# Denominators and three heads' numerators in one product, the general path off SyncE's queue, and the first loads in other halves

## The chip, the cores and the metric

The kernel runs on one core of one Trainium2 chip. The metric is the device time of one execution in microseconds; the kernel before has a median of 270.71 us over 3 runs (270.58 to 271.08). The engines are TensorE (PE in the profile; PEld is its weight load), VectorE (DVE), ScalarE (ACT), GpSimd (POOL) and SyncE (SP), which here only issues DMAs and waits.

## The reference

All arrays are bf16. The input x has 2048 rows of 512. Two branches are computed from it and mixed by a gate per row.

```python
x = A_x
g = _sigmoid((x * gate_w).sum(-1, keepdims=True))
a = _A_ref(x, A_wq, A_wk, A_wv, A_wo, A_beta)
b = _B_ref(x, B_w_gate, B_w_up, B_w_down)
return g * a + (1 - g) * b
```

Branch B is a gated feed-forward block: gelu(x w_gate) times (x w_up), 1792 wide, then w_down. Branch A is attention with a memory, 32 heads of 16 dimensions, over four segments of 512 rows:

```python
logits = jnp.einsum('bhqd,bhkd->bhqk', qs, ks) * scale + mask
p = _softmax(logits, axis=-1)
a_dot = jnp.einsum('bhqk,bhkd->bhqd', p, vs)
pq = phi(qs)
num = jnp.einsum('bhld,bhde->bhle', pq, M)
den = jnp.einsum('bhld,bhd->bhl', pq, z)[..., None] + 1e-06
a_mem = num / den
o = g * a_mem + (1.0 - g) * a_dot
...
pk = phi(ks)
M = M + jnp.einsum('bhld,bhle->bhde', pk, vs)
z = z + jnp.einsum('bhld->bhd', pk)
```

Here phi(t) is t + 1 for positive t and exp(t) otherwise, the mask is causal within the segment, and g is a sigmoid of one beta per head. The first segment has an empty memory.

## The kernel before, in words

The kernel keeps the transposed x of a segment (512 features over 128 partitions and four chunks `fc`, by 512 rows) and forms from it K, Q (transposed, eight heads in each of four groups `c`), V, the gate and the up branch. Every such product is one unit of TensorE work: four matmuls of 512 columns into one PSUM bank, followed by one read of the bank by VectorE or ScalarE. The pool `gen` has four such banks for all units; four more banks hold the logits. Attention runs in 72 visits: in each, `group_qk` (L612) forms 2048 columns of logits, ScalarE takes their exponential, GpSimd masks the diagonal blocks, and two visits after its last block a group's `pv` (L632) multiplies by V into a pair of banks, which VectorE transposes, normalises and turns back.

The order of all other work is made at build time by a planner. Streams of units (K, Q, V, gate, up, down, output, memory) carry a wanted visit, a condition, and a cost in TensorE and VectorE time; `fill_to` (L746) takes the unit with the smallest wanted visit, corrected by a modelled backlog of VectorE, until the next exponential is due. `later(n, f)` (L312) runs a step n visits on, and `passed(pe, dve)` (L692) books its modelled time. Each engine then executes its instructions in the order in which they were written down.

The memory: after a segment, `u_pk` (L386) transposes phi(K) by DMA, `u_M` (L523) adds phi(K)ᵀ[V 1] to the accumulator `Macc`, and `u_mask` (L542) writes the block-diagonal copies: `Mz` (8 columns per group, for the denominators) and, two and eight visits later, the halves of `Mn` (128 columns per group, eight heads of 16). `u_den` (L563) multiplies phi(Q) by `Mz` for two groups at a time, eight matmuls of 8 columns into one bank `zd`; VectorE adds 1e-6 out of the bank at once, and one visit later `f_inv` takes the reciprocal and multiplies by g. `mem_num` (L596) multiplies phi(Q) of one group by `Mn`, four matmuls of 128 columns into a bank `mn`; VectorE multiplies by the reciprocals into `tm`, and a DMA on SyncE's queue transposes it for `add_mem`. This is done for three segments and four groups.

The head: `load_inputs` (L134) issues on SyncE's queue x's first segment in two halves, wk in two halves of its columns, wq, the gate vector, wv and the gate weights. `transpose_x0` (L175) transposes x on TensorE; VectorE and ScalarE copy it out. Then, before the planner starts, three K units, four Q units, the gate vector's transpose, four V units and the gate units follow one another. Each of the first three K units is cast by VectorE, which also writes its two masked copies `KTm` (L378); VectorE casts Q and V too.

The end: the kernel has a general path (`general`, L1066) for inputs whose logits could overflow. A flag `safe` is computed from absolute maxima; its value is loaded into a register of every engine at L1129, and all engines branch at L1130. In this execution the general path is not taken. Its DMAs (x, transposes, V, output) are all on SyncE's queue.

```python
    ok = nc.values_load(safe[0:1, 0:1])
    with tc.If(ok == 0, preferred_fallthrough_block=True, label="safe"):
        general()
```

Of the kernel before, what the change touches and what calls it, by code (L numbers as in the profile page):

```python
# [11 lines left out]
ALU = mybir.AluOpType  # L12

P = 128
D = 512
# [15 lines left out]
DV = HV * DH  # L31
BF = dt.bfloat16
# [21 lines left out]
def kernel(  # L54
# [47 lines left out]
    Mn = [const([P, NC8, 128], BF, f"Mn{i}") for i in range(2)]  # L102
    Mz = [const([P, NC8, 8], BF, f"Mz{i}") for i in range(2)]
# [23 lines left out]

    def x_seg(s):
        nc.sync.dma_start_transpose(xS[s % NX][:, :, :], x2[s * L:(s + 1) * L, :])
# [45 lines left out]
    def transpose_x0():  # L175
        for half in range(2):
            for f0 in range(0, FC, 2):
                T = pgen.tile([P, 1024], BF, name="x0T", tag="gen")
                for i in range(4):
# [3 lines left out]
                dst = xS[0][:, f0:f0 + 2, half * 256:half * 256 + 256].rearrange(  # L183
                    "q f (p k) -> q f k p", k=2)
                src = T[:, 0:512].rearrange("q (f k p) -> q f k p", f=2, k=2)
# [177 lines left out]

    def u_k(s, c):
        def f():
            T = gen("kT")
            for fc in range(FC):
                nc.tensor.matmul(T[:, :], lhsT=wk[:, fc, c * P:(c + 1) * P],  # L368
                                 rhs=xS[s % NX][:, fc, :],
                                 start=(fc == 0), stop=(fc == FC - 1))  # L370
                if fc < FC - 1:
                    yield MM512
            cast(ktb[:, c, :], T[:, :])
            if general_now[0]:
                return MM512
            for p in range(2):
                eng = nc.vector if s == 0 and c < NK else nc.gpsimd
                eng.tensor_scalar(out=KTm[:, (NC8 * s + c) % NK, :, p, :],  # L378
                                  in0=ktb[:, c, :].rearrange("q (b k) -> q b k", b=NB),
                                  scalar1=eo[:, p:p + 1], scalar2=None, op0=ALU.mult)  # L380
            return MM512
        return 4 * MM512, EVAC, f

    pk_at = {}

    def u_pk(s, c):  # L386
        def f():
            assert ("k", s, c - c % 2) in ready
            nc.sync.dma_start_transpose(pk[:, :, c * P:(c + 1) * P], ktb[:, c, :])
# [55 lines left out]
    def u_vs(s):  # L445
        def f():
            v, w = V[s % 2], Vs[s % 2]
            nc.sync.dma_start(w[0:64, :, 0:VE], v[64:128, :, 0:VE])
            nc.sync.dma_start(w[64:128, :, 0:VE], v[0:64, :, VE:2 * VE])
# [55 lines left out]
    def u_out(s, qt):  # L505
        def f():
# [12 lines left out]
            nc.sync.dma_start(out2[q0:q0 + P, :], osb)  # L519
# [22 lines left out]
    def u_mask(s):  # L542
        def half(h0):
            nc.vector.tensor_tensor(
                out=Mn[s % 2][:, h0:h0 + 2, :].rearrange("p c (h e) -> p c h e", h=8),
# [5 lines left out]
        def f():  # L551
# [3 lines left out]
            nc.vector.tensor_tensor(out=Mz[s % 2][:, :, :], in0=Macc[:, :, :, 16],  # L555
# [6 lines left out]

    def u_den(s, pair):  # L563
        def f():
            assert general_now[0] or ("q", s, 2 * pair) in ready
            T = gen("zd")
            Tv = T[:, 0:KT * 16].rearrange("p (q h) -> p q h", q=KT)
            for cc in range(2):
                c = 2 * pair + cc
                for qq in range(KT):  # L570
                    nc.tensor.matmul(Tv[:, qq, 8 * cc:8 * cc + 8],
                                     lhsT=pq[:, c, qq * P:(qq + 1) * P],
                                     rhs=Mz[s % 2][:, c, :], start=True, stop=True)
# [4 lines left out]
            nc.vector.tensor_scalar_add(r, Tv, 1e-6)  # L578

            def f_inv():  # L580
# [4 lines left out]
                passed(0.0, 0.8)  # L585
# [7 lines left out]

    tms = {}

    def mem_num(s, c):  # L596
        assert general_now[0] or (count(("Mn", s)) > c // 2 and count(("inv", s)) > c // 2)
        T = gen("mn")
        for qq in range(KT):
            nc.tensor.matmul(T[:, qq * P:(qq + 1) * P],  # L600
                             lhsT=pq[:, c, qq * P:(qq + 1) * P], rhs=Mn[s % 2][:, c, :],
                             start=True, stop=True)
        tm = wk2.tile([P, KT, 8, DH], BF, name="tm", tag="tm")
# [556 lines left out]
```

## Time and profile before

| | |
|---|---|
| median of 3 runs | 270.71 us (270.58 to 271.08) |
| the profiled execution | 270.57 us, of which span 268.84 us |
| TensorE busy | 262.3 us (98%), granted clock 0.996 |
| VectorE, ScalarE, GpSimd busy | 203.7 (76%), 209.0 (78%), 156.8 us (58%) |
| first K product starts | 5.83 us, after a wait for wk |
| numerators L600 | 48 of 128 columns; multiply L604 12 times 686 ns |
| denominators L571 | 48 of 8 columns |
| last VectorE instruction of the output | ends 265.4 us |
| end of the span | 268.8 us |

Times are microseconds from the start of the span unless marked ns. In a timeline line the first number is the start and the second the time until the last instruction of the merged group ended, so a group of pipelined matmuls is longer than its starts are apart; the bracket gives the idle time before it and what ended that. In a view of one source line, the three numbers after the count are the shortest, median and longest duration in ns, followed by the first and last start. A q behind an engine's name marks its instruction queue: waits, branches and DMA issues.

### The profile page before, as it was taken

To read this page: it belongs to the slowest core of one execution; us is meant where nothing else is said; L and a number is where in the kernel's file an instruction comes from. 1 tells how busy PE (TensorE), PEld (TensorE's weight loads), DVE (VectorE), ACT (ScalarE), POOL (GpSimd) and SP (SyncE) were. 2 spreads that over 40 slices of the span, in tenths; PEclk is the share of its full clock that TensorE was granted. 3 is DMA by queue.
4 is the path that set the end of the run, shared out by engine and by line. 5 is a ranking of instruction groups with operands and counts; after the bars stand their busy time and mean duration, and the time that the engine had idled before them with its cause. 6 is when DMAs were issued, how large, how long until landed. Compare 5 with 4: busy or idle time off the path is not lost.

```text
span 268.8 us, 6576 instructions
## 1 busy us (share of the span) xinstructions
PE 262.3 (98%) x2713; PEld 117.5 (44%) x2713; DVE 203.7 (76%) x390; ACT 209.0 (78%) x163; POOL 156.8 (58%) x298
## 2 busy tenths in 40 slices
PE   7999999999999999999999999999999999999993
PEld 3454434344453444445444444444444544344441
DVE  2999575868777887697986979596898588697374
ACT  3237889999997998889999988889888987567420
POOL 4000168897905979987811998596875089654400
PEclk9999999999999999999999999999999999999998
DMA  6999901200160000301052002110000200001102
GB/s 205 334 211 321 331 18 35 41 4 0 29 136 2 0 22 22 78 4 41 0 68 56 2 21 50 33 34 8 20 24 21 66 2 20 19 3 41 39 22 85
DMA packets 30282, 16.60 MB, mean 62 GB/s; under 512 B 20008, under 2 KB 28968, under 8 KB 30248
## 3 DMA queue, kind: packets, MB, share of 16 engines
q1 hardware_dynamic: 30248, 16.14, 22.9%
q8 instruction: 22, 0.36, 0.6%
q14 instruction: 12, 0.10, 0.1%
HBM read 8.14 MB, written 2.10 MB: 38 GB/s over the span
## 4 chain that ended last, share of the span: by engine, by line
PE 86%; POOL 5%; issue 4%; DMA 2%; ACT 1%; SPq 0%; DVE 0%; ACTq 0%; DVEq 0%; POOLq 0%
PE gT L456 19%; PE uT L477 17%; PE dT L493 14%; PE lg L618 8%; PE od L643 6%; PE aT L510 5%; PE qT L282 5%; PE kT L368 5%; PE vT L397 4%; POOL pT L627 3%; POOL KTm L378 2%; DMA wk<-in_A_wk_dram 2%; PE MT L531 1%; PE mn L600 1%; ACT pT L623 1%
## 5 line engine op out<-in xcount | busy, mean ns | idle before, releaser
L627 POOL TENSOR_SCALAR_AFFINE_SELECT pT<-pT 64x256 bf16<-64x256 bf16 x256 | 113.8, 445 | 94.2 <-ACT pT L623 81.4
L623 ACT ACTIVATE pT<-lg 128x2048 bf16<-128x2048 f32 x72 | 135.1, 1876 | 24.9 <-PE lg L618 21.6
L477 PE MATMUL uT<-x,wup 128*128 128x512 bf16 x224 | 60.4, 380 | 0.0
L456 PE MATMUL gT<-x,wga 128*128 128x512 bf16 x224 | 57.0, 380 | 0.0
L493 PE MATMUL dT<-wdn,G 128*128 128x512 bf16 x224 | 52.9, 380 | 0.0
L483 DVE TENSOR_TENSOR G<-uT,G 128x512 bf16<-128x512 f32 x56 | 38.1, 684 | 6.4 <-PE uT L477 6.2
L378 POOL TENSOR_SCALAR KTm<-ktb,eo 128x512 bf16<-128x512 bf16 x26 | 40.6, 1572 | 1.3
L650 DVE STREAM_TRANSPOSE oq<-od 128x512 f32<-128x512 f32 x32 | 21.0, 695 | 19.5 <-PE od L643 19.5
L493 PEld LDWEIGHTS <-G 128*128 128x128 bf16 x224 | 20.8, 98 | 25.0 <-issue 2.1
L456 PEld LDWEIGHTS <-wga 128*128 128x128 bf16 x224 | 20.5, 98 | 23.9 <-issue 2.2
L477 PEld LDWEIGHTS <-wup 128*128 128x128 bf16 x224 | 19.8, 97 | 24.0 <-issue 5.4
L618 PE MATMUL lg<-QT,KTm 32*128 32x192 bf16 (+7 forms) x512 | 28.5, 287 | 0.0
L305 DVE CAST G<-gT 128x512 bf16<-128x512 f32 x24 | 16.5, 688 | 9.7 <-PE gT L456 9.5
L618 PEld LDWEIGHTS <-KTm 32*128 32x128 bf16 x512 | 8.3, 92 | 28.4 <-issue 28.1
L643 PE MATMUL od<-pT,V 64*32 64x128 bf16 (+7 forms) x512 | 19.4, 284 | 0.2 <-POOL pT L627 0.2
L643 PE MATMUL od<-pT,Vs 64*32 64x128 bf16 (+7 forms) x512 | 19.4, 284 | 0.0
L471 ACT ACTIVATE G<-G 128x3584 bf16<-128x3584 bf16 x6 | 18.8, 3182 | 0.0
L656 DVE SCALAR_TENSOR_TENSOR o<-oq,ogs,rden 128x256 bf16<-128x256 f32 x32 | 17.0, 532 | 1.1
L368 PE MATMUL kT<-x,wk 128*128 128x512 bf16 x64 | 16.8, 380 | 0.9 <-DMA wk<-in_A_wk_dram 0.9
L282 PE MATMUL qT<-x,wq 128*128 128x512 bf16 x64 | 16.6, 379 | 0.0
L515 DVE SCALAR_TENSOR_TENSOR tB<-aT,gct,tB 128x512 bf16<-128x512 f32 x16 | 11.9, 746 | 6.0 <-PE aT L510 5.7
L510 PE MATMUL aT<-wo,oT 128*128 128x512 bf16 x64 | 16.5, 380 | 0.0
(96 smaller groups left out, 274.8 us busy)
## 6 DMA issues: line engine op xcount, KB each, us to landing
out_dram<-tB SPq DMA_DIRECT2D x16, 128.0 KB, 1.7
wup<-in_B_w_up_dram SPq DMA_DIRECT2D x1, 1792.0 KB, 8.4
wdn<-in_B_w_down_dram SPq DMA_DIRECT2D x1, 1792.0 KB
wga<-in_B_w_gate_dram SPq DMA_DIRECT2D x1, 1280.0 KB, 10.2
Vs<-V SPq DMA_DIRECT2D x8, 144.0 KB, 2.6
G<-in_A_x_dram SPq DMA_DIRECT2D x2, 256.0 KB, 2.8
wk<-in_A_wk_dram SPq DMA_DIRECT2D x2, 256.0 KB, 4.2
wq<-in_A_wq_dram SPq DMA_DIRECT2D x1, 512.0 KB, 5.7
```

Of the source, the lines that this page charges most:

```text
L282: nc.tensor.matmul(T[:, :], lhsT=wq[:, fc, c * P:(c + 1) * P], rhs=xS[s % NX][:, fc, :], start=(fc == 0), stop=(fc == FC - 1))
L368: nc.tensor.matmul(T[:, :], lhsT=wk[:, fc, c * P:(c + 1) * P], rhs=xS[s % NX][:, fc, :], start=(fc == 0), stop=(fc == FC - 1))
L378: eng.tensor_scalar(out=KTm[:, (NC8 * s + c) % NK, :, p, :], in0=ktb[:, c, :].rearrange("q (b k) -> q b k", b=NB), scalar1=eo[:, p:p + 1], ...
L456: nc.tensor.matmul(T[:, :], lhsT=wga[:, fc, hs * P:(hs + 1) * P], rhs=xS[s % NX][:, fc, :], start=(fc == 0), stop=(fc == FC - 1))
L477: nc.tensor.matmul(T[:, :], lhsT=wup[:, fc, hs * P:(hs + 1) * P], rhs=xS[s % NX][:, fc, :], start=(fc == 0), stop=(fc == FC - 1))
L483: nc.vector.tensor_tensor(out=g, in0=T[:, :], in1=g, op=ALU.mult)
L493: nc.tensor.matmul(T[:, :], lhsT=G[s % NG][:, hs, qt * P:(qt + 1) * P], rhs=wdn[:, hs, :], start=(hs == 0), stop=(hs == HS - 1))
L510: nc.tensor.matmul(T[:, :], lhsT=oT[:, fc, qt * P:(qt + 1) * P], rhs=wo[:, fc, :], start=(fc == 0), stop=(fc == FC - 1))
L618: nc.tensor.matmul(lg[:, j, off:off + n], lhsT=KTm[rows, i % NK, b].rearrange("r p k -> r (p k)"), rhs=QT[rows, i % NC8, 64 * b:L], start= ...
L623: nc.scalar.activation(pT[:, :, :], lg[:, :, :], AF.Exp, scale=DH ** -0.5)
L627: nc.gpsimd.affine_select(out=v, in_=v, pattern=[[0, 4], [1, 64]], compare_op=ALU.is_ge, fill=0.0, base=0, channel_multiplier=-1)
L643: nc.tensor.matmul(od[p][32 * j:32 * j + 32, 64 * b:L], lhsT=w[:, 18 * h:18 * h + 32], rhs=t[rows, j, off:off + n], start=(b == 0), stop=( ...
```

## The change

- One tile `Mm` of 8 + 128 columns per group takes the place of `Mz` and `Mn`. `u_den` multiplies phi(Q) by the first 56 columns (`DN`: eight denominators and the numerators of `HD` = 3 heads) for two groups, eight matmuls of 56 columns in one bank; `mem_num` multiplies by the other 80 columns (five heads).
- `f_inv`, after the reciprocals, also multiplies the three heads' numerators of both groups out of the `zd` bank into two tiles `tm`; `mem_num` multiplies the other five heads into the same tile.
- The stream of denominators also waits until the mask's half is written and the numerators of the earlier pair are done.
- In the general path x, V and the output go through GpSimd's DMA queue, and TensorE transposes take the place of the transposing DMAs; SyncE issues nothing there, and the flag is loaded by the other four engines only.
- x's first segment is loaded with 128 consecutive rows over the partitions, two rows of 1 KB per partition and half instead of 2 KB in one piece; the copies after the transpose are contiguous. wk is loaded in two halves of its rows (1 KB pieces) instead of its columns (512 B pieces).
- `first_k` runs the first three K units together: first the products of chunks 0 and 1 for all three, then chunks 2 and 3, each followed by its casts.

```diff
+HD = 3
+DN = 8 + HD * DH
...
-    Mn = [const([P, NC8, 128], BF, f"Mn{i}") for i in range(2)]
-    Mz = [const([P, NC8, 8], BF, f"Mz{i}") for i in range(2)]
+    Mm = [const([P, NC8, 8 + 128], BF, f"Mm{i}") for i in range(2)]
...
             nc.sync.dma_start(x0[:, 2 * i:2 * i + 2, :],
-                              x2[half * i:half * (i + 1), :].rearrange("(p k) d -> p k d", p=P))
+                              x2[half * i:half * (i + 1), :].rearrange("(k p) d -> p k d", p=P))
         for i in range(2):
-            n = slice(D // 2 * i, D // 2 * (i + 1))
-            cols(wk[:, :, n], A_wk[:, n])
+            cols(wk[:, 2 * i:2 * i + 2, :], A_wk[D // 2 * i:D // 2 * (i + 1), :])
...
+    def first_k():
+        Ts = [gen("kT") for c in range(NK)]
+        for c in range(NK):
+            for _ in k_part(Ts[c], 0, c, range(0, FC // 2)):
+                pass
+        for c in range(NK):
+            for _ in k_part(Ts[c], 0, c, range(FC // 2, FC)):
+                pass
+            k_done(Ts[c], 0, c)
+
+    def turn(dst, src):
+        T = pgen.tile([P, 1024], BF, name="tT", tag="gen")
+        for i in range(KT):
+            nc.tensor.transpose(T[:, i * P:(i + 1) * P], src[:, i, :], ident[:, :])
+        nc.vector.tensor_copy(dst, T[:, 0:512].rearrange("p (i t) -> p i t", i=KT))
...
             T = gen("zd")
-            Tv = T[:, 0:KT * 16].rearrange("p (q h) -> p q h", q=KT)
+            Tv = T[:, 0:2 * KT * DN].rearrange("p (c q e) -> p c q e", c=2, q=KT)
             for cc in range(2):
                 c = 2 * pair + cc
                 for qq in range(KT):
-                    nc.tensor.matmul(Tv[:, qq, 8 * cc:8 * cc + 8],
+                    nc.tensor.matmul(Tv[:, cc, qq, :],
                                      lhsT=pq[:, c, qq * P:(qq + 1) * P],
-                                     rhs=Mz[s % 2][:, c, :], start=True, stop=True)
+                                     rhs=Mm[s % 2][:, c, 0:DN], start=True, stop=True)
...
-                passed(0.0, 0.8)
+                for cc in range(2):
+                    c = 2 * pair + cc
+                    t = wk2.tile([P, KT, 8, DH], BF, name="tm", tag="tm")
+                    tmp[(s, c)] = t
+                    scale(t, Tv[:, cc, :, 8:], s, c, 0, HD)
+                passed(0.0, 1.4)
...
+    def scale(t, src, s, c, h0, h1):
+        nc.vector.tensor_tensor(
+            out=t[:, :, h0:h1, :], in0=src.rearrange("p q (h d) -> p q h d", d=DH),
+            in1=rdm[s % 2][:, :, 8 * c + h0:8 * c + h1, None].to_broadcast((P, KT, h1 - h0, DH)),
+            op=ALU.mult)
...
-            nc.tensor.matmul(T[:, qq * P:(qq + 1) * P],
-                             lhsT=pq[:, c, qq * P:(qq + 1) * P], rhs=Mn[s % 2][:, c, :],
+            nc.tensor.matmul(Tv[:, qq, :],
+                             lhsT=pq[:, c, qq * P:(qq + 1) * P], rhs=Mm[s % 2][:, c, DN:],
                              start=True, stop=True)
...
+        tm = tmp.pop((s, c))
+        scale(tm, Tv, s, c, HD, 8)
...
-    for c in range(NK):
-        run(u_k(0, c))
+    first_k()
...
-                    lambda s=s, pair=pair: ("q", s + 1, 2 * pair) in ready)
+                    lambda s=s, pair=pair: ("q", s + 1, 2 * pair) in ready and
+                    count(("Mn", s + 1)) > pair and count(("num", s + 1)) == 2 * pair)
...
     def general():
         general_now[0] = True
+        queue[0] = nc.gpsimd
...
-    ok = nc.values_load(safe[0:1, 0:1])
+    ok = nc.values_load(safe[0:1, 0:1],
+                        engines=[mybir.EngineType.PE, mybir.EngineType.DVE,
+                                 mybir.EngineType.Activation, mybir.EngineType.Pool])
```

More of the change, by code (lines that the diff above doesn't have):

```diff
@@ L362, in u_phk, with k_part, k_done @@
         return 0.0, 0.0, f
+    def k_part(T, s, c, fcs):
+        for fc in fcs:
+            nc.tensor.matmul(T[:, :], lhsT=wk[:, fc, c * P:(c + 1) * P], rhs=xS[s % NX][:, fc, :],
+                             start=(fc == 0), stop=(fc == FC - 1))
+            if fc < FC - 1:
+                yield MM512
+    def k_done(T, s, c):
+        cast(ktb[:, c, :], T[:, :])
+        if general_now[0]:
+            return
+        for p in range(2):
+            eng = nc.vector if s == 0 and c < NK else nc.gpsimd
+            eng.tensor_scalar(out=KTm[:, (NC8 * s + c) % NK, :, p, :],
+                              in0=ktb[:, c, :].rearrange("q (b k) -> q b k", b=NB),
+                              scalar1=eo[:, p:p + 1], scalar2=None, op0=ALU.mult)
     def u_k(s, c):
@@ L366, in f @@
             T = gen("kT")
[L367 to L380, printed above, removed]
+            yield from k_part(T, s, c, range(FC))
+            k_done(T, s, c)
             return MM512
         return 4 * MM512, EVAC, f
+    def first_k():
[12 more added lines that the diff above has]
+        nc.vector.tensor_copy(dst, T[:, 0:512].rearrange("p (i t) -> p i t", i=KT))
     pk_at = {}
@@ L942, in can_num @@
     def can_num(s, c):
-        if count(("den", s)) <= c // 2 and ("q", s, c - c % 2) in ready:
+        if (count(("den", s)) <= c // 2 and ("q", s, c - c % 2) in ready and
+                count(("Mn", s)) > c // 2):
             need(("den", s), c // 2 + 1)
@@ L1073, in general @@
             if s % NX == 0:
-                x_seg(s)
+                rows = G[(s + 1) % NG][:, 0:KT, :]
+                nc.gpsimd.dma_start(rows, x2[s * L:(s + 1) * L, :]
+                                    .rearrange("(k p) d -> p k d", p=P))
+                for fc in range(FC):
+                    turn(xS[s % NX][:, fc, :].rearrange("p (k t) -> p k t", k=KT),
+                         rows[:, :, fc * P:(fc + 1) * P])
             for c in range(NC8):
```

44 lines of the change are left out of this document (25 added, 19 removed).

## The prediction

> **What bounds the kernel now.** I read the page first (busy shares, slices), then the chain that ended last, then the timeline of the three places that the change touches: the first 17 us, the memory products, the last 4 us.
>
> ```profile
> PE 262.3 (98%) x2713; PEld 117.5 (44%) x2713; DVE 203.7 (76%) x390; ACT 209.0 (78%) x163; POOL 156.8 (58%) x298
> PE   7999999999999999999999999999999999999993
> ```
>
> TensorE is busy 98% of the span; only its first slice and its last slice have holes. In the list of waits TensorE waits for another engine between 12 and 265 us never longer than 0.2 us at a time. So from about 12 us on, whatever delays TensorE or shortens its work moves the end one for one, until another engine becomes late.
>
> The head, from the timeline:
>
> ```profile
> 5.83 2.76 PE L368 MATMUL kT<-x,wk 128*128 128x512 bf16 x12 [0.91 <-DMA wk<-in_A_wk_dram]
> 6.90 0.69 DVE L305 CAST ktb<-kT 128x512 bf16<-128x512 f32 x1 [1.18 <-PE kT L368]
> 7.63 0.62 DVE L378 TENSOR_SCALAR KTm<-ktb,eo 128x512 bf16<-128x512 bf16 x2
> ...
> 8.50 3.63 PE L282 MATMUL qT<-x,wq 128*128 128x512 bf16 x16
> ...
> 10.66 2.48 DVE L305 CAST QT<-qT 128x512 bf16<-128x512 f32 x4
> ...
> 12.17 1.31 PE L397 MATMUL vT<-wv,x 128*128 128x448 bf16 x6
> ```
>
> TensorE starts K when wk lands, and from 6.90 us VectorE works without a pause (cast, two masked copies, three times over, then the Q casts). There are four PSUM banks for all of this; the ninth tile, the first vT, takes the bank of the second qT, whose cast ends at 10.66 + 0.60 + 0.68 = 11.95 us. vT starts at 12.17: VectorE is only 0.2 us ahead of TensorE here.
>
> The memory products, from the timeline:
>
> ```profile
> 74.96 0.65 PE L413 MATMUL zT<-wv,x 128*128 128x65 bf16 x16
> 75.45 0.34 PE L571 MATMUL zd<-Mz,pq 128*128 128x8 bf16 x8
> 75.65 1.24 PE L456 MATMUL gT<-x,wga 128*128 128x512 bf16 x5
> ...
> 97.28 0.39 PE L600 MATMUL mn<-Mn,pq 128*128 128x128 bf16 x4
> ...
> 97.50 0.38 PE L368 MATMUL kT<-x,wk 128*128 128x512 bf16 x1
> ```
>
> Starts tell the pace: 16 products of 65 columns in 0.49 us (30 ns each), 8 of 8 columns in 0.20 us (25 ns), 4 of 128 columns in 0.22 us (56 ns).
>
> The end, from the views of lines 1129, 1130 and 1155, and of SyncE's waits:
>
> ```profile
> L1129 SPq TENSOR_LOAD <-safe x1: 543/543/543, 265.8 to 265.8; - x1
> L1130 SPq COMPARE_BRANCH  x1: 58/58/58, 266.4 to 266.4; - x1
> L1130 SPq EVENT_SEMAPHORE  x8: 17/17/17, 266.9 to 267.5; - x8
> L1155 SPq EVENT_SEMAPHORE  x10: 17/28/28, 267.5 to 268.8; - x10
> SPq L1130 <- SPq L1130: 0.5, 1, 0.5
> ```
>
> After the last output DMA (issued at 265.41, 0.33 us long) SyncE alone is still walking: flag load, branch, 0.5 us of nothing, eight steps of DMA semaphores for the path not taken, then the closing waits. The other engines are through the branch by 266.7 us.
>
> **The change part by part.** The sum is made against the profiled execution: 270.57 us (span 268.84 and 1.73 around it), 0.14 below the median of the three runs (270.71).
>
> *56 and 80 columns.* 48 pairs (3 segments, 4 groups, 4 tiles of queries) of 25 + 56 = 81 ns become 56 + 80 columns. 56 lies between the rows of 8 and 65 columns (25 to 30 ns), I take 27; 80 lies between 65 and 128 (30 to 56), by a straight line 36. So 63 ns, and 48 x 18 = 0.86 us less on TensorE, which is the path. Bounds: 55 ns (-1.25 us) and 86 ns (+0.24).
>
> *More, smaller VectorE multiplies.* 12 products of 512 elements (0.686 us each) become 12 of 192 and 12 of 320. The casts out of PSUM took 0.28 us at 128 elements, 0.62 at 448 and 0.69 at 512, which gives 0.35 and 0.48: 0.15 us more each, 1.8 us in all. VectorE is idle 24% of the time, so I cost it at nothing; without that cover it is +1.8.
>
> *The held bank.* Before, the zd bank is free after the add (0.2 us). Now it holds three heads' numerators until the multiplies that follow the reciprocal, which is emitted one visit later: den and reciprocal stood 6.6, 6.2, 4.3, 2.6, 1.6 and 2.0 us apart (75.4 to 82.1, 108.9 to 115.1, 143.8 to 148.1, 173.4 to 175.9, 202.5 to 204.1, 237.7 to 239.7). For that time three banks are left. I laid TensorE's tiles against the ends of their reads. In five windows three banks hold all that is alive. In the second an od pair (PV at 112.1 us) takes two at once: the gT at 113.63 would wait for the first od transpose (114.08), 0.45 us, and the uT at 115.79 for the cast behind the reciprocal, about 0.4. That is 0.85 us for a window with a PV in it. The planner now books 1.4 instead of 0.8 for the reciprocal's step and may place units otherwise, so I take 0.5; bounds 0 and 2.6 (three windows). The den's new conditions (mask done, two numerators done) were met in all six places already, and the numerators' transposing DMAs had landed before the next multiplies; nothing there waits longer.
>
> *Loads.* x's first halves go from 2 KB to 1 KB packets, wk's halves from 512 B to 1 KB. The DMA view gave 367 GB/s in the stretch of x (2.4 to 3.4 us), 268 in that of wk (4 to 5) and 331 in that of wq (6.2 to 8.4, 1 KB). So x's 512 KB lands 0.15 us later, each wk half is 0.19 shorter: first half at 5.78 + 0.15 - 0.19 = 5.74, second about 6.33, wq about 8.24 instead of 8.46. The transposed copies are done at 5.62 and 5.82 and become contiguous, so they are no later. TensorE starts K about 0.05 us sooner (bounds: 0.3 sooner, 0.15 later).
>
> *K in halves of the contraction.* The 12 products (0.216 us apart) end at 8.37 instead of 8.43. But the first K tile is finished by the eighth product instead of the fourth: 4 x 0.216 = 0.86 us later. VectorE's unbroken row starts at 5.78 + 7 x 0.216 + 0.38 + 0.04 = 7.71 instead of 6.90 and reaches the end of the second Q cast 5.05 us later, at 12.76. vT then starts at about 12.78 instead of 12.17: +0.6 us, and behind it VectorE keeps ahead again (0.6 us per cast against 0.76 per vT). Bounds: +0.35 with wk early, +0.75 with x late, and -0.1 if the bank does not bind.
>
> *The end without SyncE.* The flag load (0.54), branch (0.06), gap (0.47) and eight steps (0.6) leave SyncE's queue; what then holds its closing waits is the last output's landing, 1.7 us after 265.41 = 267.1. POOL gets the steps of its own DMA queues (the output, Vs and x rows of the general path are now its): from 266.46, eight more of 0.07 to 0.09 us, so 267.1 too. SyncE gets some four more closing waits of 0.06. It reaches its first drain at about 267.5 instead of 268.03: -0.55 us. Bounds: -0.85 (all waits met by 267.1) and +0.3 (POOL's branch over a longer block takes TensorE's 0.39 us instead of 0.05). No transfer of this execution changes its queue.
>
> Sum: 270.57 - 0.86 + 0.5 + 0.6 - 0.55 = 270.26, say 270.3 us.
>
> **The rivals.**
> 1. *The head loses nothing.* If K starts 0.3 us sooner or the ninth tile finds another bank, the head gives about -0.1. For it: TensorE did wait 0.91 us for wk. Against it: the wait of vT on VectorE's count and only 0.2 us of room. With a held bank costing 0.2: 270.57 - 0.86 + 0.2 - 0.1 - 0.55 = 269.3.
> 2. *The held bank decides.* Place: a PV pair inside a window; price 0.85 us each. From 1.7 us on, two windows, the kernel is slower by over 0.2% (-0.86 + 0.6 - 0.55 + 1.7 = +0.9). With three: 270.57 - 0.81 + 2.55 = 272.3. For it: VectorE is already the late one in such stretches (a uT finished at 113.8 was read until 116.6), and its step grows by 0.7 us. Against it: only one of six windows had a PV inside.
> 3. *The columns' split gives nothing on TensorE*, because the spacing includes the load of new weights (98 ns each, in front of every product) and is a straight line in the columns; then 8 + 128 costs what 56 + 80 does, and the time is 270.26 + 0.86 = 271.1. The rows of 25, 30 and 56 ns speak against it: 8 columns and 65 differ by 5 ns only, 65 and 128 by 26. The Trainium skill, TensorE: Matmul & The Clock Gate, section Back-to-back issue gap, gives such a line for a stream of loads and products, 81 ns at 128 columns and 131 at 512; by it the estimate is 146 ns for either pair. The trace has 56 and 216 and does not agree.
>
> **How the numbers follow.** A measurement of this kernel can tell about 0.2%, 0.54 us, from no change. My forecast gets 0.42 (own range 269.6 to 271.0; faster 0.13, same 0.24, slower 0.05), rival 1 0.30 (all faster), rival 2 0.22 (all slower), rival 3 0.06 (same 0.04, slower 0.02). Together faster 0.43, same 0.28, slower 0.29. The range leaves out what of rival 1 adds the 55 ns pair and of rival 2 more than three windows, under 0.2 in all: 269.0 to 272.3.
>
> **What would show it.** Right: products of 56 and 80 columns at 27 and 36 ns; the first K cast near 7.7 us and vT near 12.8; SyncE without flag load and branch, its first drain near 267.5 less what the rest moved. Wrong: vT before 12.3 us (the head gains); holes in TensorE between den and the multiplies in more than one window; POOL's branch longer than 0.3 us; a different order of units between visits that makes VectorE late elsewhere.

## The result, and the profile after

The changed kernel takes 272.61 us (median of six runs, 272.15 to 272.79); the kernel before, run beside it, 271.02 us (270.58 to 271.15). The ratio is 1.0055, with a 95% interval of 1.004 to 1.007: 1.6 us slower. The profiled execution of the changed kernel took 272.53 us with a span of 270.70, against 270.57 and 268.84.

The page of the changed kernel, busy shares and TensorE's slices:

```profile
PE 258.4 (95%) x2674; PEld 117.6 (43%) x2713; DVE 204.7 (76%) x404; ACT 207.7 (77%) x161; POOL 157.0 (58%) x298
PE   7899999999999999999999999999999999999993
```

The page hardly tells that anything happened. (TensorE's busy sum is no measure here: 39 product records are missing from this trace, as the two counts show.) VectorE's share is still 76%, though its 203.7 us became 204.7 and its instructions 390 became 404. So the places have to be looked at one by one, those of the prediction first.

The first 14 us, from the timeline of the changed kernel:

```profile
6.04 2.76 PE L367 MATMUL kT<-x,wk 128*128 128x512 bf16 x12 [0.63 <-DMA wk<-in_A_wk_dram]
7.97 0.69 DVE L306 CAST ktb<-kT 128x512 bf16<-128x512 f32 x1 [2.20 <-PE kT L367]
8.64 3.63 PE L283 MATMUL qT<-x,wq 128*128 128x512 bf16 x15
11.73 2.48 DVE L306 CAST QT<-qT 128x512 bf16<-128x512 f32 x4
12.47 0.16 PE L194 MATMUL gwT<-ident,G 4*128 4x4 bf16 x1 [0.20 <-DVE QT L306]
13.07 3.19 PE L422 MATMUL vT<-wv,x 128*128 128x448 bf16 x16 [0.44 <-DVE QT L306]
```

VectorE now stands idle for 2.20 us until the first K bank is finished (7.97 instead of 6.90), its row of casts comes 1.07 us later, and TensorE waits for it twice, at 12.47 and 13.07. The first V product starts 0.90 us later than before.

The memory products, from the same view:

```profile
76.34 0.37 PE L598 MATMUL zd<-Mm,pq 128*128 128x56 bf16 x8
76.55 1.89 PE L481 MATMUL gT<-x,wga 128*128 128x512 bf16 x7
...
98.17 0.31 PE L641 MATMUL mn<-Mm,pq 128*128 128x80 bf16 x4
98.31 0.38 PE L367 MATMUL kT<-x,wk 128*128 128x512 bf16 x1
```

Eight products of 56 columns take 0.21 us from start to start of what follows, four of 80 columns 0.14. In the raw starts the spacing is 26 and 35 ns, against 25 and 56 before.

The second of the six windows between a denominator product and the multiplies, first TensorE, then VectorE:

```profile
114.35 0.38 PE L502 MATMUL uT<-x,wup 128*128 128x512 bf16 x1 [0.16 <-issue]
115.07 0.81 PE L481 MATMUL gT<-x,wga 128*128 128x512 bf16 x3 [0.34 <-DVE oq L692]
117.56 1.02 PE L502 MATMUL uT<-x,wup 128*128 128x512 bf16 x4 [0.17 <-DVE tm L628]
...
114.30 1.31 DVE L692 STREAM_TRANSPOSE oq<-od 128x512 f32<-128x512 f32 x2 [1.33 <-PE od L685]
115.54 0.49 DVE L706 TENSOR_TENSOR oT<-oT,mT 128x512 bf16<-128x512 bf16 x1
115.95 0.54 DVE L609 RECIPROCAL rdm<-rdm 128x64 f32<-128x64 f32 x1
116.52 0.32 DVE L610 TENSOR_TENSOR rdm<-rdm,gh 128x64 f32<-128x64 f32 x1
116.88 0.62 DVE L628 TENSOR_TENSOR tm<-zd,rdm 128x192 bf16<-128x192 f32 x2
117.42 0.68 DVE L508 TENSOR_TENSOR G<-uT,G 128x512 bf16<-128x512 f32 x1
```

The gT at 115.07 waits until the first od transpose gives its bank back, the uT at 117.56 for the multiplies out of the held zd bank (ended 117.50). The bracket's 0.34 and 0.17 count from the modelled end of the product before; from start to start, 114.35 to 115.07 is 0.72 where a product of 512 columns has 0.216, so 0.50 and, in the same way, 0.33 are lost.

VectorE's multiplies, from the groups by line:

```profile
L628 DVE TENSOR_TENSOR tm<-mn,rdm 128x320 bf16<-128x320 f32 x12 | 5.8, 484 | 2.9 <-PE mn L641 2.7
L628 DVE TENSOR_TENSOR tm<-zd,rdm 128x192 bf16<-128x192 f32 x12 | 3.7, 352 | 0.2
```

Together they keep VectorE busy for 9.5 us (5.8 and 3.7; two multiplies in a row overlap by a little), against 12 times 686 ns, 8.2 us, before. The end, from the views of lines 1181 and 1206 (the branch and the closing waits) and of SyncE's waits:

```profile
L1181 POOLq INC_SWDGE_SEM  x1: 177/177/177, 268.8 to 268.8; - x1
L1181 DVEq EVENT_SEMAPHORE  x1: 21/21/21, 269.6 to 269.6; - x1
L1206 SPq EVENT_SEMAPHORE  x14: 17/28/168, 269.0 to 270.6; - x14
SPq L1206 <- DVEq L1181: 0.2, 1, 0.2
```

SyncE has no flag load and no branch left. But its closing waits (the semaphore steps at the end of the program) begin only at 269.0, right behind GpSimd's last step for the queues of the path not taken (268.8), there are 14 of them instead of 10, and one waits 0.17 us for VectorE.

Where the 1.86 us of span come from, in three stretches. Call the lag of a visit the time by which its exponential starts later than in the kernel before, and the loop the stretch of the 72 visits. The lag of the first exponential is 0.89 us, and it stays as it is through the first 23 visits. From there to the flag (`safe`, 265.29 before, 267.26 after) another 1.08 us are lost, although each of the 12 numerator products makes the lag 0.08 smaller, 0.96 in all; what was lost against them is therefore 2.04 us, and 1.0 of it at visits 30 and 31, in the window shown above. From the flag to the end of the span it is 3.44 instead of 3.54 us, 0.10 gained.

### The profile page after: what moved, and what is told of

The parts are those of the page before. It is cut to its first block, busy times and chain, and to the rows that moved or that the text cites. A ratio compares the mean times of both kernels' runs of the same rounds, so it can differ in the third digit from the quotient of the medians.

```text
span 270.7 us, 6538 instructions
## 1 busy us (share of the span) xinstructions
PE 258.4 (95%) x2674; PEld 117.6 (43%) x2713; DVE 204.7 (76%) x404; ACT 207.7 (77%) x161; POOL 157.0 (58%) x298
## 4 chain that ended last, share of the span: by engine, by line
PE 76%; DVE 8%; issue 6%; POOL 5%; DMA 2%; ACT 1%; SPq 0%; ACTq 0%; DVEq 0%; POOLq 0%
PE gT L481 16%; PE uT L502 15%; PE dT L518 14%; PE lg L660 7%; PE od L685 6%; PE aT L535 5%; PE kT L367 4%; PE vT L422 4%; POOL pT L669 3%; PE qT L283 3%; POOL KTm L378 2%; DMA wk<-in_A_wk_dram 2%; ACT pT L665 1%; DVE oq L692 1%; DVE o L698 1%
## 5 line engine op out<-in xcount | busy, mean ns | idle before, releaser
L502 PE MATMUL uT<-x,wup 128*128 128x512 bf16 x211 | 57.6, 380 | 1.8 <-issue 1.3
L481 PE MATMUL gT<-x,wga 128*128 128x512 bf16 x211 | 55.1, 379 | 1.9 <-issue 1.3
L518 PE MATMUL dT<-wdn,G 128*128 128x512 bf16 x218 | 52.2, 380 | 0.7 <-issue 0.6
L306 DVE CAST G<-gT 128x512 bf16<-128x512 f32 x23 | 15.8, 689 | 9.9 <-PE gT L481 9.7
L685 PE MATMUL od<-pT,V 64*32 64x256 bf16 (+7 forms) x512 | 19.8, 284 | 0.2 <-POOL pT L669 0.2
L685 PE MATMUL od<-pT,Vs 64*32 64x256 bf16 (+7 forms) x512 | 19.1, 284 | 0.2 <-DMA Vs<-V 0.2
```

The costliest lines, as they stand in the source:

```text
L481: nc.tensor.matmul(T[:, :], lhsT=wga[:, fc, hs * P:(hs + 1) * P], rhs=xS[s % NX][:, fc, :], start=(fc == 0), stop=(fc == FC - 1))
L502: nc.tensor.matmul(T[:, :], lhsT=wup[:, fc, hs * P:(hs + 1) * P], rhs=xS[s % NX][:, fc, :], start=(fc == 0), stop=(fc == FC - 1))
L518: nc.tensor.matmul(T[:, :], lhsT=G[s % NG][:, hs, qt * P:(qt + 1) * P], rhs=wdn[:, hs, :], start=(hs == 0), stop=(hs == HS - 1))
L685: nc.tensor.matmul(od[p][32 * j:32 * j + 32, 64 * b:L], lhsT=w[:, 18 * h:18 * h + 32], rhs=t[rows, j, off:off + n], start=(b == 0), stop=( ...
```

## The experiments

The first question was which of the three parts costs, the second why. My first theory was that the planner's new order of units (it differs from before at 117 us, where a gate unit and a V unit stand later, and from 149 us on) cost most of the loop's 2 us; the rivals were the held bank and VectorE's work.

**The head alone.** The loads and `first_k`, with the rest as before.

```diff
-            n = slice(D // 2 * i, D // 2 * (i + 1))
-            cols(wk[:, :, n], A_wk[:, n])
+            cols(wk[:, 2 * i:2 * i + 2, :], A_wk[D // 2 * i:D // 2 * (i + 1), :])
...
-    for c in range(NK):
-        run(u_k(0, c))
+    first_k()
```

> The kernel before with the head's part of the change alone (x and wk loads, contiguous copies, K in halves of the contraction); TensorE's order of the units after the head is that of before. Theory A (the trace of the changed kernel): vT starts 0.9 us later because the first K cast starts 1.07 us later, and nothing behind it makes that up: +0.9 us. Rival B (the head's delay is swallowed later): within 0.2 us of the kernel before.

Measured: 271.61 us (271.34 to 271.84) beside 270.77, ratio 1.0034 (1.0021 to 1.0046): +0.84. The head is a loss of its own.

**The end alone.** The general path off SyncE's queue, flag load without SyncE.

> The kernel before with the end's part alone (general path without SyncE, flag loaded by four engines). Theory A: SyncE's closing waits now start behind GpSimd's stand-in for its own DMA semaphores, so only 0.1 us is won: -0.1 us. Rival B (the forecast's term): -0.55 us; the 0.1 us in the changed kernel's trace would then come from something that the other parts do to the end.

Measured: 270.59 us (270.31 to 271.12), ratio 0.9991 (0.9982 to 1.0): -0.18. From the flag to the end it is 3.30 us instead of 3.54. In this kernel VectorE's branch (266.76) and its next step (267.37) are 0.6 apart, against 1.6 in the changed kernel, and no closing wait is long:

```profile
L1192 SPq EVENT_SEMAPHORE  x14: 17/28/28, 267.7 to 269.2; - x14
```

The 14 steps, more than before, eat a part of the gain: between the first closing wait and the first drain lie 0.7 us here (267.7 to 268.4) and 0.5 before (267.5 to 268.0). (The drain is the instruction that follows these waits on SyncE.)

**The columns alone.** 56 and 80 columns with all that they bring, head and end as before.

> The kernel before with the columns' part alone: 56 and 80 columns, held bank, the planner's 1.4. TensorE's order is that of the changed kernel. Theory A: what is left of the changed kernel's loss after head and end, +0.7 to +1.1 us. Rival B (the parts hurt only together): -0.3 us or better, as forecast.

Measured: 271.77 us (271.43 to 272.28), ratio 1.0041 (1.0028 to 1.0055): +1.0. The three parts make 0.84 - 0.18 + 1.00 = 1.66; the whole is 1.59. They add.

**The columns, with the planner told what it was told before.** The step of the reciprocals books 0.8 instead of 1.4 us; then TensorE's order of products is that of the kernel before.

```diff
-                passed(0.0, 1.4)
+                passed(0.0, 0.8)
```

> As the one before, but the planner books 0.8 for the reciprocal's step, as in the kernel before; every unit of TensorE then stands in the order of the kernel before. Theory A (the new order costs the most of it): the held bank's one stall of 1.0 us and the shorter products of -0.96 us cancel, so +0.1 us, and 0.7 to 1.0 us less than with 1.4. Rival B (the held bank costs all of it, whatever the order): within 0.2 us of the kernel with 1.4.

Measured: 271.60 us (271.15 to 271.98), ratio 1.0040 (1.0026 to 1.0054): +0.83. With the same order most of the loss is still there, so the theory that the order costs most of it falls; the 0.17 between the two kernels lies within their ranges. The traces leave the order a smaller share: from the first to the last exponential the lag grows by 1.16 us with the new order and by 0.71 with the former one. This trace gives the loop term by term: twelve times -0.08, then +0.65 and +0.30 at visits 30 and 31, and +0.11, +0.19 and +0.28 at visits 41, 66 and 71 and a remainder of 0.14 in smaller steps: +0.71 in all. The waits behind these steps have different ends: at visit 30 the first od transpose, at visits 31, 41 and 71 VectorE's multiplies into `tm`, at visit 66 a mask of GpSimd (the PV's products on both sides of that wait start 0.46 us apart, and 0.27 in the kernel before).

**The head with two Q casts on ScalarE.** As the head alone, but the first two Q banks are read by ScalarE instead of VectorE.

```diff
-            cast(QT[:, c, :], T[:, :])
+            if act:
+                nc.scalar.copy(QT[:, c, :], T[:, :])
+            else:
+                cast(QT[:, c, :], T[:, :])
```

> The head's part alone, and the casts of the first two Q tiles given to ScalarE, which is idle between 6 and 11 us there. Theory A (the first vT waits for VectorE's row of casts, which starts late): the wait before vT goes, 0.6 to 0.8 us faster than the head's part alone, so 0 to +0.2 against the kernel before. Rival B (the late landing of wk is what costs): still +0.7 or more.

Measured: 270.92 us beside 270.86, ratio 1.0012 (0.9996 to 1.0029): the loss is gone. Its timeline:

```profile
11.86 1.28 DVE L306 CAST QT<-qT 128x512 bf16<-128x512 f32 x2
12.41 1.31 PE L419 MATMUL vT<-wv,x 128*128 128x448 bf16 x6
```

VectorE's row is as late as in the changed kernel (11.86 for the first Q cast), but vT follows without a wait. So it is VectorE's row of casts that holds the ninth bank, as the prediction had it.

**Only the order of the first K units**, loads as before.

> Only the order of the first three K units is changed (halves of the contraction); loads and copies are those of the kernel before. Theory A: VectorE's row starts 0.86 us later and vT, which had 0.2 us of room, 0.65 us later: +0.65 us. Rival B (the loads are what costs): within 0.2 us of the kernel before.

Measured: 271.66 us (271.35 to 272.14), ratio 1.0028 (1.0016 to 1.004): +0.80 by the medians, as much as order and loads together. The loads give and take nothing that shows.

**The held bank alone.** The kernel before with its 8 and 128 columns, but the addition of 1e-6, the only read of the zd bank, is moved behind the visit, in front of the reciprocal.

```diff
-            nc.vector.tensor_scalar_add(r, Tv, 1e-6)
...
             def f_inv():
+                nc.vector.tensor_scalar_add(r, Tv, 1e-6)
                 nc.vector.reciprocal(r, r)
```

> The kernel before, its columns untouched, but VectorE's add out of the zd bank stands in the later step beside the reciprocal, so the bank is held one visit longer with no work added and no unit moved. Theory A (the held bank stops TensorE at the PV that falls into the second window): two waits of TensorE near 113.6 and 115.8 us, together 0.7 to 0.9, and up to 0.3 elsewhere: +0.7 to +1.1 us. Rival B (the extra multiplies of VectorE are what stops TensorE): within 0.2 us of the kernel before.

Measured: 271.43 us (median) beside 270.86, ratio 1.0031 (1.0017 to 1.0045), less than expected. The loop's whole loss is one step of 0.65 us at visit 30 and nothing in the other five windows:

```profile
113.70 0.38 PE L477 MATMUL uT<-x,wup 128*128 128x512 bf16 x1 [0.16 <-issue]
114.42 0.81 PE L456 MATMUL gT<-x,wga 128*128 128x512 bf16 x3 [0.34 <-DVE oq L650]
```

It is the same gT with the same 0.50 us; the second wait, of the uT, did not come. Here the bank is free after the addition at 115.48 us, in front of the reciprocal, while in the changed kernel it is held through the reciprocal and the multiplies. So held until the reciprocal the bank costs in one window, and that is not enough for the 1.67 us that the loop lost with the columns alone (0.71 + 0.96).

**The columns without a held bank.** VectorE copies the three heads' numerators out of the zd bank right after the addition and multiplies them later from SBUF; order as before.

```diff
+            st = wk2.tile([P, 2, KT, HD * DH], BF, name="st", tag="st", bufs=1)
+            nc.vector.tensor_copy(st[:, :, :, :], Tv[:, :, :, 8:])
...
-                    scale(t, Tv[:, cc, :, 8:], s, c, 0, HD)
+                    scale(t, st[:, cc, :, :], s, c, 0, HD)
```

> 56 and 80 columns with the order of the kernel before, but VectorE copies the three heads' numerators out of the zd bank right behind the add (384 elements, about 0.55 us, six times), and the later multiplies read the copy. Theory A: the bank is free as before, the waits near 113 us go, and the shorter products stay: 0.8 to 1.0 us faster than the same columns with the bank held, so 0 to -0.3 us against the kernel before (VectorE has 3.3 us more to do). Rival B (VectorE's work is the cause): no faster than with the bank held, +0.8 us or more.

Measured: 272.53 us (272.09 to 273.07) beside 270.86, ratio 1.0066 (1.0054 to 1.0079): +1.67, worse by 0.8 than with the bank held. No bank is held, and yet TensorE waits in the same place, now for the uT's multiply that stands behind the reciprocals on VectorE:

```profile
117.43 0.38 PE L457 MATMUL gT<-x,wga 128*128 128x512 bf16 x1 [0.99 <-DVE G L484]
```

The uT's multiply stands there behind the reciprocal and two multiplies, and another 1.1 us are lost at visits 70 and 71. The six copies took 548 ns each, and the multiplies out of SBUF were dearer too: VectorE is busy 6.4 us more with these steps than before (3.3 for the copies, 5.5 and 5.8 instead of 8.2 for the multiplies), where the change has 1.3. So the second suspect, VectorE's work, which I had costed at nothing, costs without a held bank, but this kernel has far more of it than the change.

**VectorE's work alone.** TensorE's products and the bank as before; VectorE multiplies twice 192 elements behind each reciprocal and 320 instead of 512 elements behind each numerator product. Its result leaves out the first three heads' numerators.

```diff
-                    scale(t, Tv[:, cc, :, 8:], s, c, 0, HD)
+                    scale(t, dum[:, :, :], s, c, 0, HD)
...
-        scale(tm, Tv, s, c, HD, 8)
+        scale(tm, Tv[:, :, HD * DH:], s, c, HD, 8)
```

> TensorE's products are those of before (8 and 128 columns), no bank is held, and the order is that of before. Only VectorE's work is the change's: behind each of the six reciprocals it multiplies twice 192 elements (out of a constant tile in SBUF, so the first three heads' numerators are left out of the result), and the numerators' multiply takes 320 elements instead of 512. Theory (VectorE's moved work costs by itself where VectorE is late, as in the staged kernel): about +0.7 us behind the reciprocals where the next PSUM bank waits for VectorE, +0.3 to +1.0 in all over the kernel before. It also follows from a sum: booked as before, the loop gave +0.71, less -0.96 for the products and +0.65 for the held bank leaves +1.0. Rival (only the bank costs, and the extra work costs only in the held window): 0.0 to +0.2.

Measured: 272.69 us (272.32 to 273.0) beside 270.79, ratio 1.0068 (1.0055 to 1.0081): +1.9, more than expected. Out of the constant tile a multiply took 458 ns in the mean instead of 352, but not evenly: 544 to 578 ns in the first, second and sixth window and 348 to 358 in the others, as out of the bank. So this overstates the work by 0.4 us in the second window (1.06 us for the two instead of 0.62) and again in the last segment. The place is again the second window (TensorE and VectorE of this kernel's timeline):

```profile
118.04 0.38 PE L459 MATMUL gT<-x,wga 128*128 128x512 bf16 x1 [0.95 <-DVE G L486]
...
113.64 1.31 DVE L667 STREAM_TRANSPOSE oq<-od 128x512 f32<-128x512 f32 x2 [1.19 <-PE od L660]
114.87 0.60 DVE L681 TENSOR_TENSOR oT<-oT,mT 128x512 bf16<-128x512 bf16 x1
115.40 0.54 DVE L587 RECIPROCAL rdm<-rdm 128x64 f32<-128x64 f32 x1
116.33 1.06 DVE L606 TENSOR_TENSOR tm<-dum,rdm 128x192 bf16<-128x192 f32 x2
117.31 0.68 DVE L486 TENSOR_TENSOR G<-uT,G 128x512 bf16<-128x512 f32 x1
```

Behind the PV's transposes VectorE has no idle time until 121 us; the 1.06 us of new multiplies stand in front of the multiply that frees the uT's bank, and TensorE loses 1.1 us there. Another 0.8 us are lost from visit 66 on, in the last segment. In the loop the held bank alone costs 0.65 and VectorE's work alone 1.74, or about 0.9 without the 0.4 us too much in each of the two places, which is an estimate. Both together cost 1.67, in the kernel with the columns and the order of before. In the second window they don't add: 0.65 and, by the same estimate, 0.7 alone, but 0.95 together, since TensorE waits for the same row of VectorE either way.

**The work given to other engines.** ScalarE copies the numerators out of the bank, GpSimd multiplies them; VectorE then has 2.4 us less to do than before.

```diff
-            nc.vector.tensor_copy(st[:, :, :, :], Tv[:, :, :, 8:])
+            nc.scalar.copy(st[:, :, :, :], Tv[:, :, :, 8:])
...
-                    scale(t, st[:, cc, :, :], s, c, 0, HD)
+                    scale(t, st[:, cc, :, :], s, c, 0, HD, nc.gpsimd)
```

> The columns' part alone, in the order of before, but ScalarE copies the three heads' numerators out of the bank right after the product (six copies of 384 elements, about 0.5 us each) and GpSimd multiplies them from SBUF (12 of 192 elements). No bank is held and VectorE has 2.4 us less to do (12 multiplies of 484 ns instead of 686). Theory (the bank and VectorE's work are what ate the products' gain): 269.5 to 270.1, that is 0.8 to 1.4 us less than before. Rival: ScalarE's copies delay six exponentials by 0.5 us each and GpSimd's multiplies delay the masks behind them, and TensorE waits for these instead: 270.6 to 271.5.

Measured: 273.98 us (273.24 to 274.84), ratio 1.0112 (1.0092 to 1.0133). Even the rival was too kind. 4.0 us are lost in one place, the first window (the timeline, first ScalarE, then TensorE):

```profile
72.50 6.27 ACT L472 ACTIVATE G<-G 128x3584 bf16<-128x3584 bf16 x2
80.08 1.88 ACT L640 ACTIVATE pT<-lg 128x2048 bf16<-128x2048 f32 x1
81.85 0.47 ACT L584 CAST st<-zd 128x384 bf16<-128x384 f32 x1
...
82.38 4.22 PE L494 MATMUL dT<-wdn,G 128*128 128x512 bf16 x11 [2.16 <-ACT st L584]
```

Two stretches of the same kernel, by engine (length, then busy us and instructions of PE, PEld, DVE, ACT and POOL, then the granted clock, the DMA share and GB/s):

```profile
80.20:82.30 2.10, 0.02 (x1) 0.00 (x0) 2.01 (x5) 2.10 (x2) 0.28 (x1) 1.00 0.00 0
82.30:84.50 2.20, 2.12 (x6) 0.85 (x6) 0.65 (x2) 0.03 (x1) 1.37 (x4) 0.55 0.00 0
```

The denominators are ready at 75.9, but ScalarE's copy stands behind two gelu instructions of 3.2 us each, a table load and an exponential. The bank is held 6 us, TensorE has nothing to write to for 2.16 us, and behind that hole its clock is halved: the eleven products take 4.15 us from start to the next start, 0.38 each instead of 0.216. In the other windows it gains 0.88 on the products and loses 1.1, so even without that stall this would be no gain.

**The same with the change's end.**

> The kernel with ScalarE's copies and GpSimd's multiplies and the change's end (general path off SyncE's queue) in one. If the parts add, 0.2 us less than that kernel: 269.3 to 269.9 by the theory, 270.4 to 271.3 by the rival. Were the end's gain an accident of one kernel, the two would be equal.

Measured: 274.22 us (274.1 to 274.35), ratio 1.0128 (1.0114 to 1.0143): the same stall, and by the medians no 0.2 us gained that would show; neither branch of the expectation was met, since both stood on the kernel above. In the trace the end did gain: from the flag to the end of the span it is 3.05 us, against 3.56 in the kernel above. Counted from the flag, GpSimd's last step came 0.24 us sooner than in the kernel with the end alone (1.35 instead of 1.59 us), and SyncE's first closing wait did so too (1.47 instead of 1.71). So it is GpSimd's steps that these waits stand behind.

**The columns, multiplied at once.** What was left open was whether VectorE's work costs by its amount or by its place. Here the reciprocals and the three heads' multiplies are written right behind the addition, not one visit later; the planner's order and bookings are those of before.

```diff
-            def f_inv():
+            def f_mul():
                 nc.vector.reciprocal(r, r)
...
+            f_mul()
             if general_now[0]:
                 f_inv()
```

> The columns' part alone with the order of before, but the reciprocals, the product with g and the three heads' multiplies are written right behind the add instead of one visit later. The bank is then held about 1.9 us instead of 2 to 7, and in the second window VectorE does this near 110 to 112 us, where it stood idle for 0.5, 0.2 and 1.2 us, and not behind the PV at 115. Theory (the place of VectorE's extra work costs, behind a PV and in the last segment, not its amount): the -0.96 of the products comes through: 269.7 to 270.2. Rival (the amount costs, wherever it stands, as VectorE is late somewhere in each segment): as with the multiplies one visit later, 271.3 to 271.7.

Measured: 270.67 us (270.52 to 270.99) beside 270.85, ratio 0.9983 (0.9965 to 1.0001). That is 1.0 us less than with the multiplies one visit later (271.60 beside 270.77), so the place was worth that, together with the shorter hold of the bank, which comes with it and which no run separates from it. But it is not the 0.96 of the products below before: over the loop the lag changes by only +0.05 us. The steps: twelve times -0.08, against +0.45 at visit 30, +0.20 at 66, +0.20 at 71 and a few smaller. The one at 71 is a wait for VectorE's multiply of a numerator. The one at 66 is not VectorE's: the PV waits for a mask of GpSimd there, its products on both sides of the wait start 0.47 us apart and 0.27 in the kernel before. The 0.45 (VectorE, then TensorE), and last TensorE's wait at visit 66:

```profile
110.80 0.86 DVE L607 TENSOR_TENSOR tm<-zd,rdm 128x192 bf16<-128x192 f32 x2
111.58 0.68 DVE L306 CAST G<-gT 128x512 bf16<-128x512 f32 x1
...
111.86 0.39 PE L661 MATMUL od<-pT,V 64*32 64x512 bf16 x1
112.31 0.39 PE L661 MATMUL od<-pT,Vs 64*32 64x512 bf16 x1
...
228.58 0.29 PE L661 MATMUL od<-pT,V 64*32 64x320 bf16 x1 [0.17 <-POOL pT L645]
```

Now the cast of a gT stands behind the multiplies, and the PV's second bank is free only when it ends, at 112.26.

**The reciprocals at once, in the kernel before**; and both of these **with the change's end**.

> The kernel before, with only the reciprocals and the product with g (0.9 us of VectorE, six times) moved right behind the add; order and products as before. It shows what of the former kernel's time is the place alone. Theory: VectorE is late for TensorE only by fractions there, so 0.0 to -0.3: 270.5 to 270.8. Rival (the moved steps delay the casts behind the denominators): +0.2 to +0.5.

Measured: 270.87 us beside 270.85, ratio 1.0008 (0.9986 to 1.0031); over the loop the lag moves by 0.03 us. The former place cost nothing as long as there was only the reciprocal.

> The columns' part with the multiplies at once, and the change's end (general path off SyncE's queue), without the change's head. If the parts add, 0.2 us below the columns' part alone: 269.5 to 270.0 by the theory that the place costs, which would be below both kernels; 271.1 to 271.5 by the rival that the amount costs.

Measured: 270.50 us (270.18 to 270.80), ratio 0.9981 (0.9966 to 0.9995).

> The products of before (8 and 128 columns), the reciprocals at once, and the change's end. Against the kernel with 56 and 80 columns, the same place and the same end it shows what the split itself is worth once nothing is held for long: theory 0.7 to 1.0 us for the split, so this one at 270.3 to 270.7. Rival (the split's gain on TensorE is taken back by 1.3 us more of VectorE): no difference between the two.

Measured: 270.63 us (270.13 to 270.95), ratio 0.9984 (0.9969 to 1.0). The first of the two is the fastest kernel of this study, 0.35 us below the kernel before, where the changed one was 1.6 above it. But the split is no visible part of it: 0.13 us lie between them, less than either interval, and in both traces the loop takes as long as before (+0.04 and +0.01). What there is to gain is the end without SyncE: in all five kernels that have it, the stretch from the flag to the end is 3.05 to 3.44 us, and 3.54 to 3.57 in the twelve others. So both readings hold half: the later place, with the longer hold, costs 1.0 us, and at the earlier place VectorE's amount takes back most of what the products give (0.65 us in two steps), a wait for GpSimd another 0.2.

## Why the prediction was wrong

I said 270.3 us, between 269.0 and 272.3. It is 272.6, outside of the range, and on the side that I gave 0.29. In the profiled executions the span grew by 1.86 us, where the sum had -0.31.

- **56 and 80 columns: right.** 26 and 35 ns were measured, 27 and 36 taken; 12 times 0.08 = 0.96 us, against 0.86. The rival of a straight line in the columns falls. The Trainium skill, TensorE: Matmul & The Clock Gate, section "Wait — 56ns, not 53.3ns?", states a floor of about 25 ns from start to start for small products; the two traces agree (25 ns at 8 columns before, 26 at 56 after). The Trainium skill, TensorE: Matmul & The Clock Gate, section Back-to-back issue gap, states about 81 ns at 128 columns for a stream of loads and products; the numerators of before stand 56 ns apart at 128 columns and do not agree.
- **More, smaller VectorE multiplies, "costed at nothing": this is the step that failed.** The amount was as worked out (352 and 484 ns instead of 686, 0.15 us more each), and in busy time even less (1.3 us instead of 1.8). But the price of a cover that is gone, which I put at that amount and then left out, was taken from a mean: VectorE is idle 24% of the span and not at all for the 7 us behind the PV of the second window. And the change doesn't only add 1.3 us. It takes 0.2 us from each numerator's multiply, where VectorE waits for TensorE, and adds 0.6 us in one piece behind each reciprocal, where in the second window and the last segment TensorE waits for VectorE. On top of the bank held until the reciprocal, the loop lost another 1.0 us with the multiplies (1.67 and 0.65 with the order of before); that includes the longer hold of the bank until they end and 0.19 us of waiting for GpSimd. The work alone cost 1.7 us with multiplies that took too long, about 0.9 by the estimate above.
- **The held bank: right in mechanism and place, and the working in size; the term of the sum was too small.** The working had 0.45 for the gT and 0.4 for the uT, in the second window only. Measured: 0.50 and 0.33. I then wrote 0.5 because the planner might place units otherwise; held until the reciprocal alone it costs 0.65, and the uT's wait comes only with the multiplies. The rival of three such windows has a time near the measured one, but for a wrong reason: one window has a PV inside and such a price (in the third the bank costs about 0.1 us). Bank and multiplies together lost 1.67 us with the order of before and 2.04 in the changed kernel, the new order included, where the sum had 0.5. That is 1.5 of the 2.2 us that were missed; the rest is 0.3 in the head and 0.45 at the end, less the 0.1 that the products gave beyond the forecast.
- **K in halves: right.** From the first K product to the first vT the forecast is 12.78 - 5.78 = 7.00 us; it is 7.03 in the changed kernel, 6.34 before. In the eleven traces with the former order whose K products run at full pace (12 in 2.75 to 2.81 us) it is 6.24 to 6.54; in the two other traces with the new order and no cast moved, whose K products were slower (2.89 and 2.94 us), it is 7.16 and 7.21. The rival that the head loses nothing falls.
- **Loads: not confirmed.** K started 0.2 us later, not 0.05 sooner. But with the former loads K started anywhere from 5.65 to 6.18 us in fourteen traces, and order and loads together cost no more than the order alone. The 0.2 us say nothing of the loads, and I should have taken nothing for them.
- **The end without SyncE: right in sign, mis-sized.** -0.10 in the changed kernel's trace, -0.18 by the medians of the part alone, -0.55 in the sum. SyncE's closing waits do begin 0.5 us sooner behind the flag (1.7 instead of 2.2 us), when GpSimd has come to its last step. The sum let 0.4 us pass from there to the first drain; it was 0.88, since all twelve waits before the drain stand behind the beginning of GpSimd's last step, and one of them waited for VectorE.

## What to carry to other kernels

An engine's idle share is no cover: look for its idle time in the microseconds behind the place where the work lands, and ask who waits for what stands next in its queue. Work that is split into a later and an earlier piece is two changes; the piece that moves to where the engine is late can cost its full length, and the piece taken from where it waits anyway need not save anything. A gain on the bounding engine counts only as far as the engines that free its buffers and make its operands can follow.

## What was not expected of the hardware

- A hole of 2.16 us in TensorE's work is followed by some 3 us at half the clock (the granted clock is 0.50 in each half microsecond from 83.0 to 85.5 us in the kernel with ScalarE's copies, and 1.00 from 86.0), which makes the hole cost 4.0 us. The Trainium skill, TensorE: Matmul & The Clock Gate, section HAM oscillation — how this bites in real kernels, warns of gaps above about 3.4 us; here 2.16 us were enough.
- A multiply of 192 elements out of PSUM took 346 to 359 ns, beside whatever GpSimd did. Out of SBUF, in bf16 or f32, it took 348 to 359 ns in some windows and 544 to 578 in others (means 494 and 458). The long ones all ran beside GpSimd's masks; those beside its steps for `KTm` were short. No run here shows why the masks cost and the other steps don't. Copying out of a bank first made the multiply itself dearer in four of six windows, besides the copy.
- VectorE's step behind a branch that isn't taken came 0.6 us later in the kernel with the end alone and 1.6 us later in the changed kernel. Why is open; in the changed kernel one closing wait of SyncE took 0.14 us longer for it.
